# Mode rows loaded straight into TensorE's operand tiles, and two differences moved from VectorE to GpSimd

## The chip, the cores and the metric

The kernel runs on one core of a Trainium2 chip. The metric is the device time of one execution in microseconds. A core has TensorE (PE) for matmuls, VectorE (DVE), ScalarE (ACT) and GpSimd (POOL) for elementwise work, and SyncE (SP), which here only issues DMAs. Each engine works through its own instructions strictly in the order in which the program holds them.

## The reference

Four layers act on a sequence of 2048 steps and 512 channels: A, B, A, B, each on the layernorm of x and with a residual.

```
x = x + A(layernorm(x), k, v, shift_k, ssm_k, ssm_D)   # y = fftconv(kv, ssm_k) + kv*ssm_D;  q * y
x = x + B(layernorm(x), log_A_real, A_imag, C, log_dt, D_skip)
x = x + A(...)                                         # the same weights again
x = x + B(...)                                         # the same weights again
# inside B, for each of 512 channels and 128 modes:
P = exp((A * dt)[:, :, None] * arange(2048))           # A = -exp(log_A_real) + i*A_imag
K = 2 * einsum("dn,dnl->dl", C * dt, P).real           # the long kernel, then fftconv(u, K)
```

The kernel of B, K, is computed from modes: for each channel and mode there is a magnitude (the logarithm of |C|, and the decay per step) and a phase (the angle of C in turns, and the rotation per step).

## The kernel before, in words

The sequence is cut for an FFT of length 4096 that is done by matmuls with constant matrices (`w1`, `w2`, `mm`, `w4`). Work falls into three parts.

1. **The head**, written out directly. Four arrays `la`, `ai`, `cr`, `ci` (128 partitions x 512) hold the modes' parameters. From them the head makes four row arrays: decay `la`, rotation `ai`, phase `ph` and log magnitude `t2`. The helper `split(i, v, eng)` writes each of them as a high part (cast to fp32r on ScalarE) and a low part (the difference `v - high`, on the engine that is given) into a tile `hl`, and stores `hl` into the DRAM arrays `rows_d[0]` (phases) and `rows_d[1]` (magnitudes), in a layout in which PE can contract over parts and channels.
2. **The planned part**, called A below. Every instruction is recorded first and given an order by the class `Planner`, which plays the instructions through with a cost for each and takes at each step the one that can start first. Two generators are interleaved here. `stream()` makes K: 16 groups of modes (index `gi`), each in four taps `k`. `load_rows(gi)` fetches the rows of a group; `mags` multiplies them by tables and takes the exponential (tile `m`, PSUM tile `pm`); `angles` makes the phase in turns (PSUM tile `pa`), where DVE rounds it (`y`) and PE subtracts the rounded part; `waves` takes the sines (`tt`); `products` makes `xy` on GpSimd and `e2` on DVE; `contract` sums over modes (`pk`), scales (`ks`) and stores `kdram`. `diagonal()` does layer A: the products `prod` of k, v and the shift taps on GpSimd, summed on PE into `kv`, multiplied on DVE and stored to `kv_d`; the spectra (`kk`, `pf`, `zk`, `pu`, `pc`, stored in `spec`); row statistics of x (`xr`, `st`, `mv`, `nm`, `var`) and the convolution (`kab`, `vv`, `sw`, `pi`, `w`, `po`). `wk` is the pool of the stream's tiles.
3. **Three more layers**, after the plan's end at about 500 us: B, an A-type update without a new convolution (its result `ya_d` is read again), and B, in program order.

In `load_rows` two DMAs on SP's queue bring a group's phase rows and magnitude rows into a tile `raw` of type fp32; one copy on DVE makes `rw` of type fp32r from it, which PE reads as the stationary operand. `raw` and `rw` have two buffers each. Since `hl` was already of type fp32r when it was stored, the copy changes no bit that matters; it gives the tile the type that PE's operand needs. Group `gi + 1` is asked for when group `gi` starts.

The planner's `cost` knows a lock between DVE and GpSimd: for DVE it holds for an operation with two big operands in SBUF, and not for a copy. Its order is written out once, when the program is built; on the chip, nothing is reordered.

In the profile, L177 is the helper that records an instruction outside the plan, and L342 the line that writes out the planned ones; so the tiles' names tell the instructions apart, not the lines.

Of the kernel before, what the change touches and what calls it, by code (L numbers as in the profile page):

```python
# [9 lines left out]
F32 = mybir.dt.float32  # L10
F32R = mybir.dt.float32r
# [342 lines left out]
def kernel(ctx: ExitStack, tc: tile.TileContext, out, x_in, kv_in, ssmk_in, ssmd_in,  # L354
# [4 lines left out]
    V, S, G, T, Q = [planner.engine(e) for e in "VSGTD"]  # L359
    after = planner.after  # L360

    def sbuf(stack, name, side="left"):
        return stack.enter_context(tc.tile_pool(name=name, bufs=1, side=side, reuse_waits="tile"))
# [8 lines left out]
    rows_d = [dram.tile([NQ, 128, 4, 128], F32, name=f"rows_d{k}") for k in range(2)]  # L372
# [254 lines left out]
    def split(i, v, eng):  # L627
        k, r = divmod(i, 2)
        hl = nat.tile([128, 2, 4, 128], F32R, name="hl", tag="hl", bufs=4)
        S.copy(hl[:, 0], v)  # L630
        eng.tensor_sub(hl[:, 1], v, hl[:, 0])
        Q.dma_start(rows_d[k].rearrange("q (h r x) g n -> r (q h) x (g n)", h=2, r=2)[r]
                          .rearrange("a (c p) y -> a c (p y)", p=2),
                          hl.rearrange("p s g n -> p (s g n)").bitcast(F32))

    bits = lambda t_: t_.bitcast(I32)
    t0, t1, t2, t3, ph = [nat.tile([128, 4, 128], F32, name=n, tag=n) for n in ("t0", "t1", "t2", "t3", "ph")]
# [42 lines left out]
    V.tensor_mul(ph, ph, t0)  # L680
    V.scalar_tensor_tensor(ph, ph, -0.125, cr, op0=ALU.add, op1=ALU.mult)
    V.scalar_tensor_tensor(ph, ph, 0.25, ci, op0=ALU.add, op1=ALU.mult)
    split(1, ph, V)
    split(3, t2, V)
    S.activation(warm, t2[:, 0, 0:1], AF.Exp, scale=0.0)
    tabs = {}
    for key, w_, src in (("tg2", 32, tg2_in), ("tg1", 64, tg1_in), ("tt", 64, tt_in)):
# [15 lines left out]
    wk = sbuf(gctx, "wk")  # L703
# [10 lines left out]
    rows, ms, xys, pks, angs = {}, {}, {}, {}, {}  # L714
# [5 lines left out]
    def load_rows(gi):  # L720
        if gi in rows:
            return
        raw = wk.tile([128, 2, 128], F32, name="raw", tag="raw", bufs=2)
        q, g = divmod(gi, 4)
        for k in range(2):
            Q.dma_start(raw[:, k, :], rows_d[k][q, :, g, :])
        rows[gi] = wk.tile([128, 2, 128], F32R, name="rw", tag="rw", bufs=2)
        V.tensor_copy(rows[gi], raw)

    def mags(gi, s, col):  # L730
        pm = wide("pm")
# [79 lines left out]

    def taps():
        load_rows(0)
        load_rows(1)

        def exps(gi):
# [4 lines left out]
        for n in range(64 + LP + LC):  # L821
            gi, k = divmod(n, 4)
            if n < 64:
                if k == 0:
                    if gi > 0 and gi < 15:
                        load_rows(gi + 1)
                    if EORD == 1:
                        exps(gi)
                    elif EORD == 3 and gi % 2 == 0:
                        exps(gi)  # L830
                        exps(gi + 1)
                if n == XN:
                    root = normalizer(0, 16, lambda t: st0[:, t, :])
                    after(root, last_exp[0])
                    last_exp[0] = root
                    G.tensor_scalar(off, nm, -1.0, None, op0=ALU.mult)
                angles(gi, k)
                waves(gi, k)
            if 0 <= n - LP < 64:
                products(*divmod(n - LP, 4))  # L840
            m = n - LP - LC
            if 0 <= m < 64:
                contract(*divmod(m, 4))
                if m % 16 == 15:
                    todo.append(spectrum_quarter(1, m // 16, kdram, kp, zlast_k, 1))
            yield
# [381 lines left out]
```

## Time and profile before

| | |
|---|---|
| median of 3 runs | 748.78 us (744.72 to 751.23) |
| profiled execution: its own time | 749.08 us |
| profiled execution: span on the core | 747.2 us |
| mean granted TensorE clock | 0.877 |
| DVE instructions, POOL instructions | 918, 342 |
| head | about 0 to 34 us |
| planned part (A and the making of K) | to about 500 us |
| B, update, B | 500 to 747 us |

Rows of a timeline read: start in us, duration in us, engine, line, operation, output <- input, shape, count of merged instructions, and in brackets how long the engine sat idle before and what ended that. SPq is the queue of DMA issues on SP: its duration is the issue, together with what the queue waited for between merged issues.

### The profile page before, as it was taken

The numbers are of one execution on the slowest core, as the hardware profiler recorded it, in microseconds if no ns is written. First come the engines' busy times: TensorE is split into PE (matmuls) and PEld (weight loads), VectorE is DVE, ScalarE is ACT, GpSimd is POOL, SyncE is SP. The second block draws the span as 40 slices with busy tenths as digits, with TensorE's granted clock in tenths as the row PEclk, the third lists the DMA queues.
The fourth block names the chain that finished last, engine by engine and source line by source line (L and its number), as shares of the span: only waits on it lengthen the run. The fifth ranks groups of instructions, "written<-read, shape, count | busy, mean of one in ns | idle before, by whom it ended". The sixth has DMA issues, their size and how long they took to land. (4 is left out here: it accounts for less than half of the span.)

```text
span 747.2 us, 20838 instructions
## 1 busy us (share of the span) xinstructions
PE 553.5 (74%) x8568; PEld 307.6 (41%) x8568; DVE 508.5 (68%) x918; ACT 404.9 (54%) x768; POOL 350.1 (47%) x342
## 2 busy tenths in 40 slices
PE   1649688896798888798778789344798871589984
PEld 0114334333334434664354366122465530255662
DVE  6924965547653456578978659664588879978863
ACT  4118518655539878749445386237473326746341
POOL 3618866967756745432353053500554520254551
PEclk9988979998989659698897979876899995899998
DMA  9499858694465315565676745679686712068764
GB/s 245 121 228 236 260 153 237 182 245 125 130 197 181 132 50 150 180 210 163 199 191 232 226 124 182 171 253 277 200 283 228 253 66 104 2 212 261 250 207 93
DMA packets 74499, 138.97 MB, mean 186 GB/s; under 512 B 8092, under 2 KB 37156, under 8 KB 72356
## 3 DMA queue, kind: packets, MB, share of 16 engines
q1 hardware_dynamic: 73540, 135.21, 60.7%
q0 software_dynamic: 864, 2.43, 0.9%
q8 instruction: 68, 1.11, 0.6%
q14 instruction: 27, 0.22, 0.1%
HBM read 97.75 MB, written 39.85 MB: 184 GB/s over the span
## 5 line engine op out<-in xcount | busy, mean ns | idle before, releaser
L342 POOL TENSOR_TENSOR xy<-tt,m 128x512 f32<-128x512 f32 x128 | 148.5, 1185 | 143.9 <-ACT tt L342 64.0
L177 POOL TENSOR_TENSOR sw<-sw,kab 128x512 f32<-128x512 f32 x64 | 80.6, 1280 | 119.3 <-ACT sw L177 112.1
L342 PE MATMUL kv<-prod,minus 128*128 128x512 f32 x128 | 80.3, 720 | 9.3 <-DVE prod L342 7.1
L342 POOL TENSOR_TENSOR prod<-kvt 128x512 f32<-128x512 f32 x64 | 79.8, 1269 | 15.6 <-DMA kv_d<-prod 9.7
L342 ACT ACTIVATE m<-pm 128x1024 f32<-128x1024 f32 x48 | 46.9, 1026 | 57.8 <-PE pm L342 55.9
L342 PE MATMUL pf<-kk,w 64*128 64x512 f32 x128 | 45.0, 755 | 39.9 <-DMA kk<-ssmk_in 21.0
L342 ACT ACTIVATE ab<-pa 128x512 f32<-128x512 f32 x64 | 38.3, 599 | 61.0 <-PE pa L342 61.0
L342 DVE TENSOR_TENSOR e<-pa,m 128x512 f32<-128x512 f32 x64 | 43.6, 681 | 31.5 <-ACT pa L342 25.3
L177 DVE TENSOR_TENSOR vv<-pu,kab 128x512 f32<-128x512 f32 x64 | 40.9, 677 | 35.0 <-ACT sw L177 32.5
L177 ACT COPY ie<-pi 128x1024 f32<-128x1024 f32 x32 | 32.4, 1013 | 58.7 <-PE pi L177 58.7
L342 DVE TENSOR_SCALAR y<-pa 128x512 fp32r<-128x512 f32 x64 | 43.5, 682 | 30.0 <-PE pa L342 29.5
L177 PE MATMUL pf<-u,w 64*128 64x512 f32 (+1 forms) x136 | 40.1, 681 | 25.8 <-ACT u L177 15.8
L342 DVE STREAM_TRANSPOSE zk<-pf 128x512 f32<-128x512 f32 x64 | 41.4, 688 | 25.1 <-PE pf L342 25.1
L177 PE MATMUL pi<-vv,mm 64*64 64x128 f32 x1024 | 53.4, 276 | 1.1 <-DVE vv L177 1.1
L177 PE MATMUL pi<-sw,mm 64*64 64x128 f32 x1024 | 52.3, 270 | 1.7 <-issue 1.7
L342 PE MATMUL pa<-tt,rw 64*128 64x512 f32 x64 | 35.2, 554 | 23.1 <-DVE e L342 23.0
L342 PE MATMUL pa<-y,minus 128*128 128x512 f32 x64 | 41.9, 660 | 10.1 <-DVE y L342 10.1
L342 PE MATMUL pk<-xy,e 128*32 128x64 f32 x2048 | 47.3, 240 | 2.9 <-POOL xy L342 1.5
L177 ACT COPY sw<-pu 128x1024 f32<-128x1024 f32 x32 | 32.3, 1013 | 30.7 <-PE pu L177 30.7
L177 PE MATMUL pu<-zu,w 64*64 64x128 f32 x1024 | 37.2, 281 | 14.3 <-DVE zu L177 12.2
L342 PEld LDWEIGHTS pk<-xy,e 128*32 128x32 f32 x2048 | 36.0, 121 | 28.6 <-issue 19.8
L342 PE MATMUL pu<-zk,w 64*64 64x128 f32 x1024 | 40.0, 301 | 9.3 <-DVE zk L342 6.6
(134 smaller groups left out, 1181.1 us busy)
## 6 DMA issues: line engine op xcount, KB each, us to landing
kab<-spec SPq DMA_DIRECT2D x94, 512.0 KB, 4.6
spec<-pc SPq DMA_DIRECT2D x64, 256.0 KB, 4.3
kvt<-kv_in SPq DMA_DIRECT2D x32, 312.0 KB, 5.0
kk<-ssmk_in SPq DMA_DIRECT2D x32, 128.0 KB, 5.7
xr<-x_in SPq DMA_DIRECT2D x8, 512.0 KB, 6.6
kv_d<-prod SPq DMA_DIRECT2D x16, 256.0 KB, 3.9
kdram<-ks SPq DMA_DIRECT2D x64, 64.0 KB, 2.2
kk<-kdram SPq DMA_DIRECT2D x32, 128.0 KB, 2.8
```

The source lines that it names most:

```text
L177: op.ins = getattr(self.engines[key], name)(*a, **k).ins
L342: ins = getattr(self.engines[op.engine], name)(*a, **k).ins
```

## The change

The third argument of `split` is GpSimd instead of DVE for the rows `ph` and `t2`; the other two differences were on GpSimd already. `load_rows` lets its two DMAs write straight into `rw`, seen as fp32, and has neither `raw` nor the copy. `rw` has four buffers; `raw` and `rw` together had four.

```diff
-    split(1, ph, V)
-    split(3, t2, V)
+    split(1, ph, G)
+    split(3, t2, G)
...
     def load_rows(gi):
         if gi in rows:
             return
-        raw = wk.tile([128, 2, 128], F32, name="raw", tag="raw", bufs=2)
+        rows[gi] = wk.tile([128, 2, 128], F32R, name="rw", tag="rw", bufs=4)
         q, g = divmod(gi, 4)
         for k in range(2):
-            Q.dma_start(raw[:, k, :], rows_d[k][q, :, g, :])
-        rows[gi] = wk.tile([128, 2, 128], F32R, name="rw", tag="rw", bufs=2)
-        V.tensor_copy(rows[gi], raw)
+            Q.dma_start(rows[gi].bitcast(F32)[:, k, :], rows_d[k][q, :, g, :])
```

Because the planner plays the whole list again, the order of the planned part is a new one on every engine. In number, 16 copies and two differences leave DVE, two differences join GpSimd, and every other count stays.

On DVE, at the end of the head, stood the two differences (`hl_195` of the phases, `hl_199` of the magnitudes), then the transposes of layer A's first spectrum and the first copies:

```order
L177 SCALAR_TENSOR_TENSOR ph_148<-ph_148,ci_128 128x512
L177 TENSOR_TENSOR hl_195<-ph_148,hl_195 128x512
L177 TENSOR_TENSOR hl_199<-t2_146,hl_199 128x512
L342 STREAM_TRANSPOSE zk_229<-pf_232 128x512 x2
L342 STREAM_TRANSPOSE zk_229<-pf_238 128x512 x2
L342 SCALAR_TENSOR_TENSOR prod_234<-kv_236,kvt_233 128x512
L342 STREAM_TRANSPOSE zk_229<-pf_244 128x512 x2
L342 STREAM_TRANSPOSE zk_229<-pf_246 128x512 x2
L342 CAST rw_252<-raw_251 128x256
```

Now DVE goes from the phases to the transposes, and the two differences stand on GpSimd behind its earlier two, ahead of the first products:

```order
L177 TENSOR_TENSOR hl_165<-la_125,hl_165 128x512
L177 TENSOR_TENSOR hl_173<-ai_126,hl_173 128x512
L177 TENSOR_TENSOR hl_195<-ph_148,hl_195 128x512
L177 TENSOR_TENSOR hl_199<-t2_146,hl_199 128x512
L342 MEMSET tt0_223 128x8
L342 MEMSET tt0_223 128x16
L342 MEMSET tt1_224 128x8
L342 MEMSET tt1_224 128x16
L342 MEMSET tt2_225 128x8
L342 MEMSET tt2_225 128x16
L342 TENSOR_TENSOR kk_231<-kk_231,dr_230 1x32
L342 TENSOR_TENSOR prod_234<-kvt_233 128x512 x2
```

The first products on GpSimd (`prod`) thus stand behind all four differences, and DVE's transposes behind none.

On SP's queue the stores of `hl` are followed by loads for layer A and then by the first groups' rows. Before:

```order
L177 DMA rows_d1_103<-hl_199 8x16x1024
L342 DMA kk_245<-ssmk_in 64x1x512 x2
L342 DMA w2_108<-w2_in 128x512
L342 DMA kvt_247<-kv_in 64x1x1248 x2
L342 DMA kk_322<-ssmk_in 64x1x512 x2
L342 DMA xr_328<-x_in 64x1x2048
L342 DMA raw_251<-rows_d1_103 128x128
L342 DMA raw_253<-rows_d1_103 128x128
L342 DMA raw_251<-rows_d0_102 128x128
L342 DMA kv_d1_83<-prod_234 128x512
L342 DMA raw_253<-rows_d0_102 128x128
```

After the change the same loads stand there; the rows of a third group (`rw_301`) and the second half of `xr` have come ahead of the first groups' phase rows:

```order
L177 DMA rows_d1_103<-hl_199 8x16x1024
L342 DMA kk_245<-ssmk_in 64x1x512 x2
L342 DMA w2_108<-w2_in 128x512
L342 DMA kvt_247<-kv_in 64x1x1248 x2
L342 DMA xr_325<-x_in 64x1x2048
L342 DMA kk_319<-ssmk_in 64x1x512 x2
L342 DMA rw_251<-rows_d1_103 128x128
L342 DMA rw_252<-rows_d1_103 128x128
L342 DMA rw_301<-rows_d1_103 128x128
L342 DMA dr_318<-ssmd_in 1x128
L342 DMA xr_325<-x_in 64x1x2048
L342 DMA rw_251<-rows_d0_102 128x128
```

Further on, on DVE, two small operations on the row statistics, `nm` and `var` (128x16, from SBUF to SBUF), had a copy of rows behind them:

```order
L342 TENSOR_TENSOR e2_374<-pa_364,m2_353 128x512
L342 TENSOR_SCALAR nm_115<-mv_111 128x16
L342 TENSOR_SCALAR var_113<-mv_111 128x16
L342 TENSOR_SCALAR y_387<-pa_386 128x512
L342 TENSOR_TENSOR e2_390<-pa_370,m2_353 128x512
L342 TENSOR_SCALAR y_392<-pa_391 128x512
L342 CAST rw_406<-raw_405 128x256
```

They are still there, with a product `e2` between them, and the copy is gone:

```order
L342 TENSOR_SCALAR nm_115<-mv_111 128x16
L342 TENSOR_TENSOR e2_370<-pa_360,m2_349 128x512
L342 TENSOR_SCALAR var_113<-mv_111 128x16
L342 TENSOR_SCALAR y_383<-pa_382 128x512
L342 TENSOR_TENSOR e2_386<-pa_366,m2_349 128x512
```

## The prediction

> **What bounds the kernel now.** I read the profile page first (shares), then the planned part in stretches of 25 us, then the timelines of DVE, GpSimd, SP and PE where the edited instructions stand, and the groups of instructions by form for their prices.
>
> ```profile
> PE 553.5 (74%) x8568; PEld 307.6 (41%) x8568; DVE 508.5 (68%) x918; ACT 404.9 (54%) x768; POOL 350.1 (47%) x342
> 75.00:100.00 25.00, 14.87 (x207) 7.32 (x202) 22.48 (x26) 10.48 (x27) 17.91 (x18) 0.86 0.72 212
> 150.00:175.00 25.00, 24.70 (x254) 10.48 (x252) 12.96 (x21) 15.71 (x27) 18.58 (x20) 1.00 0.88 231
> ```
>
> No engine is full over the span. The second and third rows are two stretches of the same stage (busy us of PE, its loads, DVE, ACT, POOL; then the clock and the DMA share). In the good one PE is busy 24.7 of 25 us; in the bad one 14.9, and there DVE alone is nearly full, with 26 instructions. A bad stretch of this kind is a stall on DVE, so the question is what DVE does in it. The last instruction's chain is no help here: it can be followed back to 448 us only. But the three layers behind the planned part start from its last result, so what this part gains the end gains.
>
> The first place is the end of the head.
>
> ```profile
> 22.19 10.35 DVE L177 TENSOR_TENSOR hl<-ph,hl 128x512 fp32r<-128x512 f32 x1 [0.69 <-ACT hl L177]
> 32.46 0.73 DVE L177 TENSOR_TENSOR hl<-t,hl 128x512 fp32r<-128x512 f32 x1
> 10.39 1.25 POOL L177 TENSOR_TENSOR hl<-la,hl 128x512 fp32r<-128x512 f32 x1
> 21.97 2.48 POOL L342 TENSOR_TENSOR prod<-kvt 128x512 f32<-128x512 f32 x2
> 24.63 7.36 POOL L342 TENSOR_TENSOR prod<-kvt 128x512 f32<-128x512 f32 x6
> 53.52 8.71 POOL L342 TENSOR_TENSOR prod<-kvt 128x512 f32<-128x512 f32 x7 [9.71 <-DMA kv_d<-prod]
> 19.92 13.93 SPq L177 DMA_DIRECT2D rows_d<-hl  x3
> 33.94 4.37 SPq L342 DMA_DIRECT2D kk<-ssmk_in  x2
> 43.51 2.23 SPq L342 DMA_DIRECT2D raw<-rows_d  x3
> 53.85 1.94 ACT L342 ACTIVATE m<-pm 128x1024 f32<-128x1024 f32 x2 [31.17 <-PE pm L342]
> ```
>
> The phase difference takes 10.35 us, its twin 0.73. It lasts as long as GpSimd's run of products from 21.97 us, and ends when the run does. SP's queue stands behind it: the last stores of `hl` leave at 33 us, the loads behind them follow, the rows are asked for from 43.5 us, and ACT, idle for 31 us, gets its first exponential at 53.85. GpSimd too waits 9.7 us for a store that stands in the same queue.
>
> The second place is the copy that makes `rw`.
>
> ```profile
> L342 DVE CAST rw<-raw 128x256 fp32r<-128x256 f32 x16 | 29.7, 1854 | 5.2 <-DMA raw<-rows_d 5.2
> 85.36 9.56 DVE L342 CAST rw<-raw 128x256 fp32r<-128x256 f32 x1
> 85.13 2.48 POOL L342 TENSOR_TENSOR prod<-kvt 128x512 f32<-128x512 f32 x2
> 87.58 4.55 POOL L342 TENSOR_TENSOR xy<-tt,m 128x512 f32<-128x512 f32 x4
> 92.30 2.47 POOL L342 TENSOR_TENSOR prod<-kvt 128x512 f32<-128x512 f32 x2
> 95.67 0.76 PE L342 MATMUL pa<-tt,rw 64*128 64x512 f32 x1 [7.55 <-DVE e L342]
> 100.73 1.18 POOL L342 TENSOR_TENSOR xy<-tt,m 128x512 f32<-128x512 f32 x1 [5.70 <-PE pk L342]
> 174.37 7.02 DVE L342 CAST rw<-raw 128x256 fp32r<-128x256 f32 x1
> 182.77 1.98 PE L342 MATMUL pu<-zk,w 64*64 64x128 f32 x32 [6.10 <-DVE zk L342]
> 190.14 2.35 POOL L342 TENSOR_TENSOR xy<-tt,m 128x512 f32<-128x512 f32 x2 [8.89 <-PE pk L342]
> 198.25 6.70 DVE L342 CAST rw<-raw 128x256 fp32r<-128x256 f32 x1
> 205.70 2.02 PE L342 MATMUL kv<-prod,minus 128*128 128x512 f32 x2 [4.94 <-DVE prod L342]
> 208.79 0.24 POOL L342 TENSOR_TENSOR kk<-kk,dr 1x32 f32<-1x32 f32 x1 [3.74 <-DMA kk<-ssmk_in]
> ```
>
> Sixteen copies take 29.7 us, but three of them hold 23.3 (9.56 + 7.02 + 6.70). Each again lasts through a run of GpSimd without a gap. Behind it PE runs dry and waits for DVE, and when DVE is free GpSimd waits for PE or a load: the time is lost to all three.
>
> **The change, part by part, against the profiled execution's 749.08 us** (span 747.2 and 1.9 around it; the median shown is 0.3 below).
>
> *Start.* On GpSimd the two differences cost 1.25 us each by the row of its own difference. The last ends near 22.2 + 2 x 1.25 = 24.7 us, where DVE's ended at 33.2: the stores leave 8.5 us earlier, and the loads, the rows and the first exponential behind them. What is late next is GpSimd's first product, 3.1 us (24.7 + 0.4 of small work against 21.97); its cover is the 9.71 us in which GpSimd waits later. Without that cover the gain is 5.4. Above, it could be 12.3:
>
> ```profile
> SPq L342 <- PE pf L342: 21.8, 15, 3.8
> ```
>
> The longest of SP's waits for a forward matmul, 3.8 us, lies in the pair of loads at 33.94 us, whose matmuls DVE's stall kept back. I take 8.5, as the queue's order up to the rows is nearly the same.
>
> *The three stalls.* Without the copy DVE goes on to the next `e`, `zk` or `prod`. PE idled 7.55 + 6.10 + 4.94 = 18.6 us behind them, GpSimd 5.70 + 8.89 + 3.74 = 18.3. Not all of it goes, because PE waits for DVE there in any case.
>
> ```profile
> PE pa L342 <- DVE e L342: 23.0, 16, 7.5
> SPq L342 <- DVE rw L342: 24.0, 9, 9.0
> ```
>
> By the first row (us in total, times, longest) such a wait is 23.0/16 = 1.4 us, so 18.6 - 3 x 1.4 = 14.3; I take 14, with 0 below (if GpSimd's queue bounds the stretch) and 18.6 above. The second row is SP's queue held by the copies; now a load into `rw` waits for PE's last use four groups back, which is further away than the two of before, so I add no wait.
>
> *The other thirteen copies* are 29.7 - 23.3 = 6.4 us of DVE, whose cover is its own idle time (12 of 25 us in the good stretch). I take 0, between 0 and 6.4. DVE's 5.2 us of waiting for rows becomes PE's at the same moment, behind the same DMAs: 0. The 32 DMAs stay as they are.
>
> *Where a stall can go next.* `nm` and `var`, too, are DVE operations from SBUF to SBUF, in the same stretch.
>
> ```profile
> 120.55 2.31 POOL L342 TENSOR_TENSOR xy<-tt,m 128x512 f32<-128x512 f32 x2 [4.68 <-ACT tt L342]
> 121.90 0.99 DVE L342 TENSOR_SCALAR nm<-mv 128x16 f32<-128x16 f32 x1
> 122.81 0.16 DVE L342 TENSOR_SCALAR var<-mv 128x16 f32<-128x16 f32 x1
> 126.66 1.03 DVE L342 CAST rw<-raw 128x256 fp32r<-128x256 f32 x1
> ```
>
> Before, `nm` came in a short run and lost 0.8 us. Of the eight copies up to 205 us three met a long run, of 7.8 us in the mean: 3/8 x 7.8 = 2.9. I charge 3, between -0.8 (a gap) and 19.1 (both meet the longest).
>
> The Trainium skill, in "SBUF — State Buffer", section "Who interferes with whom", says that whichever of the two engines holds the shared port keeps it for one whole instruction. By that rule a wait would end with one GpSimd operation, about 1.2 us; the row of 9.56 us outlasts eight big ones, so the trace does not agree. By the rule the charge for `nm` would be near 0 and the sum 3 us better.
>
> *Sum:* 8.5 + 14 + 0 - 3 = 19.5 us; 749.1 - 19.5 = **729.6 us**.
>
> **The rivals.** *A, only the start is gained.* GpSimd used the stalls to run ahead, and is busy 17.9 and 18.6 of 25 us in the rows above; if its queue is the real bound, the stalls come back as its own waits. Against it: it then idles 18.3 us. 749.1 - 8.5 = 740.6.
>
> *B, the clock comes on top.* Behind each stall PE's clock is low.
>
> ```profile
> 95.00:100.00 5.00, 3.30 (x27) 1.34 (x30) 4.11 (x7) 0.00 (x0) 0.03 (x1) 0.50 0.28 87
> 100.00:105.00 5.00, 4.80 (x58) 2.39 (x51) 2.86 (x8) 1.93 (x4) 4.27 (x5) 0.67 0.58 146
> 180.00:185.00 5.00, 2.23 (x33) 1.89 (x33) 3.79 (x5) 0.19 (x1) 1.25 (x2) 0.68 0.30 106
> 185.00:190.00 5.00, 5.00 (x41) 1.97 (x41) 1.86 (x3) 2.36 (x7) 0.00 (x0) 0.63 0.89 258
> 205.00:210.00 5.00, 4.30 (x7) 1.79 (x7) 3.07 (x5) 1.75 (x5) 1.26 (x3) 0.57 0.59 170
> 210.00:215.00 5.00, 4.13 (x72) 1.97 (x70) 1.38 (x2) 2.42 (x4) 3.97 (x5) 0.74 0.84 246
> ```
>
> PE's busy time times what the clock lacks is 3.2 + 2.6 + 2.9 = 8.7 us. With no stall taken off for waits that stay: 749.1 - 8.5 - 18.6 - 8.7 = 713.3. Against it: PE's clock also falls where DVE does not stall.
>
> *C, the stall moves on: slower.* Besides `nm` and `var` the normalizer has five more small SBUF operations on DVE, behind its root. If k of the seven meet long runs, 7.8 us each come back; with 22.5 gained, the kernel is slower from k = 3, and at k = 4 it is 749.1 - 22.5 + 31.2 = 757.8. Against it: the five stand together, so that one wait serves them all, and GpSimd is filled with gaps by then.
>
> *D, the new order eats the gain.* The planner's order is new on all engines, and PE's idle time differs by stretch from 0.3 to 10.1 us in the two rows above. Over 18 stretches, 1.1 us more in each is the whole 19.5: about 749, nothing that can be measured. Against it: the rows of the head and of the first groups are nearly in the old order.
>
> **How the numbers follow.** My forecast has 0.60, A 0.15, B 0.10, C 0.07, D 0.08. The time is the first's, 729.6, its own range 720 to 740. B's end (713) and D's (749) bound the whole: 712 to 750 leaves out C, and the edges of B and D. A measurement of this kernel can tell about 1% from no change, so "faster" is below 741.6 and "slower" above 756.6. The forecast gives 0.58 to faster and 0.02 to same; A, whose 740.6 lies near the edge, 0.08 and 0.07; B 0.10 to faster; D 0.01, 0.06 and 0.01; C 0.07 to slower. Faster 0.77, same 0.15, slower 0.08.
>
> **What would show it.** In the changed profile: no `rw<-raw` group; two differences of about 1.25 us on POOL that end near 24.7 us; SP's stores of `hl` done by 26 us; ACT's first exponential near 45 us instead of 53.85; between 75 and 225 us no stretch in which DVE is full and PE below 16 of 25 us; and the load of x behind the plan near 483 us; before it is this piece of the chain that ended last (start, duration):
>
> ```profile
> 502.30 6.42 DMA x<-x_d
> ```
>
> I am wrong in the stalls if such a stretch appears with `nm`, `var` or another small DVE operation of several us in it; wrong in the start if the first exponential stays behind 50 us; wrong in the carrying over if both are as said and the plan still ends near 500 us.

## The result and the profile after

The changed kernel takes 714.44 us (median of 4 runs, 713.95 to 715.50) where the kernel before takes 749.76 (4 runs, 744.72 to 751.23): the ratio is 0.9542, interval 0.9495 to 0.9590. The gain is 35.3 us, against 19.5 forecast. The profiled execution has a span of 712.1 us, and the mean granted clock rises from 0.877 to 0.898. Ratios and their intervals, here and below, are worked out from the fast runs alone, so they can differ a little from the quotient of the medians.

The first page line (busy time, share, instructions), and the two stretches of 25 us that were shown of before, with one more (busy us of PE, its loads, DVE, ACT, POOL; the clock; the DMA share; GB/s):

```profile
PE 542.0 (76%) x8568; PEld 299.9 (42%) x8568; DVE 470.6 (66%) x900; ACT 405.4 (57%) x768; POOL 351.1 (49%) x344
```

```profile
75.00:100.00 25.00, 22.33 (x213) 8.94 (x214) 16.58 (x31) 12.64 (x22) 22.20 (x22) 1.00 0.95 292
150.00:175.00 25.00, 24.33 (x361) 12.57 (x362) 15.80 (x26) 20.01 (x51) 22.71 (x22) 1.00 0.65 202
200.00:225.00 25.00, 19.92 (x355) 11.71 (x347) 10.41 (x16) 22.54 (x51) 20.13 (x21) 0.74 0.52 170
```

The stretch from 75 us, in which DVE was full and PE busy for 14.87 us at a clock of 0.86, now has PE at 22.33 at full clock and DVE at 16.58. DVE lost 38 us of "busy" time over the span, of which the removed instructions would have needed about 6 (16 copies of 0.28 us where nothing held them, two differences of 0.73 at most): the rest was waiting that the profile counts as busy.

The instructions of the prediction's steps, from the timelines of POOL, SP's queue, ACT and DVE of the changed kernel (start, duration):

```profile
22.42 1.26 POOL L177 TENSOR_TENSOR hl<-ph,hl 128x512 fp32r<-128x512 f32 x1 [2.48 <-ACT hl L177]
23.65 1.26 POOL L177 TENSOR_TENSOR hl<-t,hl 128x512 fp32r<-128x512 f32 x1
...
20.28 5.22 SPq L177 DMA_DIRECT2D rows_d<-hl  x3
...
43.96 1.03 ACT L342 ACTIVATE m<-pm 128x1024 f32<-128x1024 f32 x1 [21.10 <-PE pm L342]
...
102.50 0.17 DVE L342 TENSOR_SCALAR nm<-mv 128x16 f32<-128x16 f32 x1
104.72 0.99 DVE L342 TENSOR_SCALAR var<-mv 128x16 f32<-128x16 f32 x1
```

The differences take 1.26 us each and end at 24.9; the stores of `hl` are issued by 25.5; the first exponential comes at 43.96 instead of 53.85; `nm` and `var` lose 0.8 us together. In the chain that ended last the load of x behind the plan stands 34.8 us earlier than the 502.30 of before, so the whole gain lies ahead of it:

```profile
467.53 6.41 DMA x<-x_d
```

### The profile page after: what moved, and what is told of

The parts are those of the page before. It is cut to its first block, busy times and chain, and to the rows that moved or that the text cites. A ratio compares the mean times of both kernels' runs of the same rounds, so it can differ in the third digit from the quotient of the medians.

```text
span 712.1 us, 20816 instructions
## 1 busy us (share of the span) xinstructions
PE 542.0 (76%) x8568; PEld 299.9 (42%) x8568; DVE 470.6 (66%) x900; ACT 405.4 (57%) x768; POOL 351.1 (49%) x344
## 4 chain that ended last, share of the span: by engine, by line
PE 34%; DVE 24%; ACT 15%; issue 7%; DMA 5%; POOL 2%; SPq 0%; DVEq 0%; ACTq 0%; POOLq 0%
PE pf L342 4%; PE kv L342 4%; PE pi L342 4%; PE pa L342 4%; PE pu L342 3%; PE pi L177 3%; ACT tt L342 3%; DMA kab<-spec 3%; PE pf L177 3%; PE pk L342 2%; DVE w L177 2%; ACT m L342 2%; DVE zu L177 2%; PE pu L177 2%; DVE vv L177 2%
## 5 line engine op out<-in xcount | busy, mean ns | idle before, releaser
L342 PE MATMUL kv<-prod,minus 128*128 128x512 f32 x128 | 75.4, 680 | 2.9 <-DMA kvt<-kv_in 1.9
L342 DVE STREAM_TRANSPOSE zk<-pf 128x512 f32<-128x512 f32 x64 | 41.6, 691 | 27.5 <-PE pf L342 27.4
L342 PE MATMUL pk<-xy,e 128*32 128x64 f32 x2048 | 45.2, 231 | 5.4 <-POOL xy L342 1.9
L342 PEld LDWEIGHTS pk<-xy,e 128*32 128x32 f32 x2048 | 34.0, 115 | 30.2 <-issue 20.7
L177 DVE STREAM_TRANSPOSE zu<-pf 128x512 f32<-128x512 f32 x64 | 41.5, 688 | 4.9 <-PE pf L177 4.7
L342 PE MATMUL pa<-y,minus 128*128 128x512 f32 x64 | 37.2, 584 | 9.0 <-DVE y L342 8.9
```

The costliest lines, as they stand in the source:

```text
L177: op.ins = getattr(self.engines[key], name)(*a, **k).ins
L342: ins = getattr(self.engines[op.engine], name)(*a, **k).ins
```

## The experiments

Because the planner plays its list again after every edit, an edit also brings a new order. In the kernels called "old order" below, the planner sees what it saw in the kernel before, and the edit is made when the instruction is written out; DVE, PE, ACT, POOL and SP then hold their rows in the order of before, with only the named rows taken out or put in. Times are medians of 4 runs unless another count is given; the kernel before took 746.5 to 747.6 beside them.

**1. The start alone.** Both differences on GpSimd, copies as before, old order.

```diff
-    split(1, ph, V)
-    split(3, t2, V)
+    split(1, ph, G)
+    split(3, t2, G)
```

> The two differences on GpSimd, the copies kept, and the order of the planned part held as before (same rows on every engine but the two). Theory P (a DVE operation that needs the port shared with GpSimd waits through GpSimd's run, and the gain is these waits): the 10.35 us wait of the phase difference goes, the first exponential starts about 10 us earlier as in the changed kernel (43.96 us), the three long copies stay: 735 to 741 us. Theory O (the new order of the plan brings most of the gain): 745 us or more. My own term for the start was 8.5 us, which gives 741.

738.36 us, ratio 0.9844 (0.9775 to 0.9914): 9 us (by the interval, 6 to 17). Timeline of ACT and of DVE in this kernel:

```profile
45.33 1.94 ACT L342 ACTIVATE m<-pm 128x1024 f32<-128x1024 f32 x2 [22.46 <-PE pm L342]
...
76.44 9.55 DVE L342 CAST rw<-raw 128x256 fp32r<-128x256 f32 x1
166.91 7.21 DVE L342 CAST rw<-raw 128x256 fp32r<-128x256 f32 x1
189.90 6.72 DVE L342 CAST rw<-raw 128x256 fp32r<-128x256 f32 x1
```

The first exponential is 8.5 us earlier, and the three stalls come back at the same places and with the same length. They belong to those places, not to chance.

**2. The copies alone.** Rows loaded straight into `rw`, the planner still counting sixteen copies, none written out; differences on DVE, old order.

```diff
-        raw = wk.tile([128, 2, 128], F32, name="raw", tag="raw", bufs=2)
+        rows[gi] = wk.tile([128, 2, 128], F32R, name="rw", tag="rw", bufs=4)
+        raw = Stand(rows[gi].bitcast(F32)[:, :, :], f"raw{gi}", 2)   # counted, no memory
...
-        V.tensor_copy(rows[gi], raw)
+        V.tensor_copy(rows[gi], raw).left_out = True
```

> The rows are loaded straight into rw (four buffers), the differences stay on DVE, and the order is held as before: the planner still counts the 16 copies, and only writes none of them out. Theory P: the 10.35 us difference at the start stays, the three long waits of 23.3 us go with the copies: 722 to 730 us, a gain near 25 rather than the 14 of my sum. Theory O: 745 us or more. Theory W (it is the step between DMA and matmul that counts, not the port): as P.

716.99 us, ratio 0.9575 (0.9495 to 0.9656): 30 us, twice what the forecast gave to the stalls and 5 us more than I expected here. The differences still wait on DVE, only otherwise divided; DVE's and POOL's timelines:

```profile
24.10 2.81 DVE L193 TENSOR_TENSOR hl<-ph,hl 128x512 fp32r<-128x512 f32 x1 [0.68 <-ACT hl L193]
26.83 8.06 DVE L193 TENSOR_TENSOR hl<-t,hl 128x512 fp32r<-128x512 f32 x1
...
26.33 0.69 POOL L361 TENSOR_TENSOR kk<-kk,dr 1x32 f32<-1x32 f32 x1
26.98 7.36 POOL L361 TENSOR_TENSOR prod<-kvt 128x512 f32<-128x512 f32 x6
```

**3. The same sixteen copies, in a form that does not wait.** Everything as before, but the copy is a multiplication by one that also writes out its sum.

```diff
-        V.tensor_copy(rows[gi], raw)
+        acc = wk.tile([128, 1], F32, name="acc", tag="acc", bufs=2)
+        V.tensor_scalar(rows[gi], raw, 1.0, 0.0, op0=ALU.mult, op1=ALU.add, accum_out=acc)
```

> The copy stays on DVE at its old place, but as a multiply by 1 that also writes its sum out, a form which I take to need no second port; order and differences as before. Theory P: each copy takes about 0.4 us and none over 1 us, and the time is that of the run without copies to within 4 us: 722 to 732 us. Theory W: the copy still stands between load and matmul and on DVE, so 745 to 750 us. If this form needs the port too, there are again copies of several us and the time stays near 749.

722.82 us, ratio 0.9658 (0.9591 to 0.9725). The group of DVE, and four of the five instances that follow the place of the first long stall:

```profile
L342 DVE TENSOR_SCALAR_CACHE_REDUCE rw<-raw 128x256 fp32r<-128x256 f32 x16 | 6.5, 409 | 5.2 <-DMA raw<-rows_d 5.2
...
116.10 0.41 DVE L342 TENSOR_SCALAR_CACHE_REDUCE rw<-raw 128x256 fp32r<-128x256 f32 x1
...
163.84 0.41 DVE L342 TENSOR_SCALAR_CACHE_REDUCE rw<-raw 128x256 fp32r<-128x256 f32 x1
179.14 0.41 DVE L342 TENSOR_SCALAR_CACHE_REDUCE rw<-raw 128x256 fp32r<-128x256 f32 x1
209.65 0.41 DVE L342 TENSOR_SCALAR_CACHE_REDUCE rw<-raw 128x256 fp32r<-128x256 f32 x1
```

All sixteen last 0.41 us, and 24.5 us are gained with the copies still between the load and the matmul. So it is the copies' waiting that costs most, not that there is a copy; whether the step itself costs some of the 6 us to experiment 2, whose interval touches this one's, was not settled. The Trainium skill, in "SBUF — State Buffer", section "Who interferes with whom", says that copies and casts can take the read and write port that DVE shares with GpSimd, and the form that writes out its accumulator cannot; these rows agree.

The same rows give the price of a stall. The kernel before has these five copies at 85.36, 126.66, 174.37, 198.25 and, from its timeline of DVE,

```profile
236.73 0.32 DVE L342 CAST rw<-raw 128x256 fp32r<-128x256 f32 x1
```

and this kernel has the first of them at 85.77. Before lags by -0.4, 10.6, 10.5, 19.1 and 27.1 us: the stall of 9.56 us cost 11.0, that of 7.02 cost 8.6 and that of 6.70 cost 8.0.

What this lag of 27.5 us consists of can be read between the first and the last of these copies (columns as above), first before, then here:

```profile
85.36:236.73 151.37, 122.48 (x1310) 56.38 (x1312) 89.80 (x118) 83.83 (x171) 105.37 (x101) 0.90 0.65 185
126.66:174.37 47.71, 44.18 (x498) 20.06 (x494) 24.25 (x39) 29.49 (x62) 39.46 (x40) 0.96 0.78 207
...
85.77:209.65 123.88, 113.77 (x1309) 52.69 (x1312) 67.86 (x122) 84.00 (x171) 105.19 (x101) 0.97 0.78 226
116.10:163.84 47.74, 44.20 (x498) 20.07 (x495) 23.66 (x41) 29.56 (x62) 39.36 (x40) 0.96 0.79 215
```

The second row of each kernel is the part in which no copy waits long: there the two take the same time. Over the whole, PE idles 28.9 us before (151.37 - 122.48) and 10.1 here, which is 18.8 us of the lag. The other 8.7 are busy time of PE (122.48 against 113.77) for the same matmuls at a lower clock: busy time times clock is about 110 us in both.

**4. Both, in the old order.** Edits 1 and 2 together.

> Both parts of the change in the old order: no copies, four buffers, the differences on GpSimd. Theory P: the gains of the two single parts add up and the order is worth little: 710 to 718 us beside 714.4 of the changed kernel. Theory O: 730 us or more, and the difference to 714.4 is what the new order brings.

708.99 us, ratio 0.9463 (0.9402 to 0.9524): 38 us, about the sum of 9 and 30, and 1 us below the range that I expected. Its median is 5 us below that of the changed kernel; with the second kernel of experiment 5, which has the same time, it is the fastest here that does the whole computation.

**5. Three of the copies put back, and the other thirteen.** On top of 4; the copies go into a tile that nobody reads, so they can cost DVE's time only.

```diff
+        op = V.tensor_copy(rows[gi], raw)
+        if gi in (3, 6, 7):        # the other kernel: not in (3, 6, 7)
+            op.instead = (junk, rows[gi].bitcast(F32))
+        else:
+            op.left_out = True
```

> Both parts in the old order (709.0 us), and put back on DVE only the three copies that waited long (groups 3, 6 and 7), writing into a tile that nobody reads: no result waits for them. Theory P with its price (a stalled DVE delays everything behind it by the stall's full length and a little more for the clock): the three last about 9.5, 7 and 6.7 us again and cost 25 to 28 us: 733 to 738 us. My sum's price (what PE idled behind them less its usual waits, 14 us): 723. Theory W (the step between load and matmul): 709 to 712.

> As the run with three copies put back, but the other thirteen: none of them met a long run of GpSimd. Theory P: none lasts over 1.5 us, and they cost what the run without copies was better than the run with copies that need no port, at most 6 us: 709 to 715 us. If one of them now falls on a long run, it shows as a copy of several us and costs its length.

With the three: 734.24 us, ratio 0.9856 (0.9782 to 0.9930), 25 us more than without. With the thirteen: 708.43 us, ratio 0.9486 (0.9411 to 0.9561), nothing. DVE's timeline of the kernel with three:

```profile
72.73 9.56 DVE L363 CAST junk<-rw 128x256 f16<-128x256 f32 x1
162.72 7.23 DVE L363 CAST junk<-rw 128x256 f16<-128x256 f32 x1
187.27 6.71 DVE L363 CAST junk<-rw 128x256 f16<-128x256 f32 x1
```

Three instructions, each of which takes 0.3 us where nothing holds it, are worth 25 us.

**6. The new order again.** The changed kernel itself, beside the two of 5.

> The changed kernel itself, beside the others on one chip, for what the new order is worth. Theory P: 712 to 716 us; the old order with both parts (709.0) is better by 3 to 7 us, and would lie between 706 and 711 here. If the order is worth nothing, 709.

715.54 us, ratio 0.9613 (0.9531 to 0.9695). The new order is about 6 us slower than the old one, both times that the two were compared (714.44 against 708.99, and 715.54 against the 708.43 of the kernel with thirteen copies); the intervals still touch.

**7. Why do three copies wait through a run, and thirteen not?** A small kernel that computes nothing of the reference: one DVE operation becomes ready amid a run of GpSimd's.

> Not the reference's work: forty-eight short sections that measure the port, output zero. In each GpSimd makes a run of seven products (128x512, about 8.5 us), or the same run with one small add behind a semaphore already met in its middle, or 28 small products (128x128), or seven memsets; one DVE operation becomes ready 1 to 2 us into the run: a copy from SBUF to SBUF, an add of two SBUF tiles, a multiply that writes its sum out, or a product of a PSUM and an SBUF tile (128x256). Theory P: copy and add last 6 to 8 us in the long run (to its end, not to the end of one product), the multiply with its sum and the product from PSUM 0.3 to 0.5 us. If the port goes over at every product's end, copy and add last 1.5 us at most. With the small add in the run they end there, at about 2 to 4 us, if a semaphore wait is what lets DVE in. Beside memsets I expect the add to be free and the copy not.

Amid seven products of 128x512 the copy and the sum of two SBUF tiles lasted 0.29 to 1.55 us, to the end of one product, not of the run, also where a small addition on all partitions stood in it: my expectation was wrong. The multiplication that writes out its sum, and the product with an operand in PSUM, waited in no case (0.42 to 0.43 us). Beside memsets the sum did not wait and the copy did (2.0 to 2.9 us, until the last of the seven). Amid 28 products of 128x128 the copy took 0.39 to 0.44 us, but the sum lasted 8.1 to 8.6 us all three times. It was let in at the 20th or 22nd product, which took 0.74 us where the others take 0.45, about 3 us ahead of the run's end (DVE, then POOL):

```profile
89.19 8.17 DVE L77 TENSOR_TENSOR y<-z,x 128x256 fp32r<-128x256 f32 x1 [1.25 <-ACT z L55]
...
96.94 0.74 POOL L69 TENSOR_TENSOR run<-a,b 128x128 f32<-128x128 f32 x1
97.64 3.33 POOL L69 TENSOR_TENSOR run<-a,b 128x128 f32<-128x128 f32 x8
```

**8. Is it the form of GpSimd's operations?** The same with products in the forms of `prod` and `xy`, and a mixture that has two additions in the form of `kk` between them.

> A small kernel that does not do the reference's work (its output is zero): 48 sections, in each of which one DVE operation becomes ready while GpSimd works through eight products of 512 elements without a gap (about 10 us). GpSimd's products have four forms: plain (two whole rows), those of `prod` (an operand repeated over the row), those of `xy` (pieces of 32 elements), and a mixture in the order that stands behind the longest stall (two `prod`, four `xy`, two `prod`). DVE's operation is a copy of 128x256 or a difference of 128x512, either waiting for ACT or standing directly behind a DVE operation that waited; each at three offsets. What is open is why the copies in the kernel wait through a whole run (9.56 us), while the copies of the first small kernel waited for one product (0.55 to 1.42 us). Theory F, GpSimd's form of access decides: plain sections 0.3 to 1.6 us again, `prod`, `xy` or mixture sections 4 to 10 us. Theory B, it matters that the copy stands behind another operation of DVE and waits for nothing itself: only the sections of that kind last 4 to 10 us, in every form. Theory M, the moment decides: long and short waits in all forms, differing by offset. Where all 48 stay below 1.8 us, none of these is it, and the question stays open.

In 47 of 48 sections the DVE operation lasted at most 1.66 us, in every form and also directly behind another DVE operation: theories F and B fall. The 48th started while such a small addition ran, and lasted to the run's end (DVE, then POOL):

```profile
498.44 7.92 DVE L89 TENSOR_TENSOR w<-a,xz 128x512 fp32r<-128x512 f32 x1
...
498.34 0.24 POOL L83 TENSOR_TENSOR run<-kvt 1x32 f32<-1x32 f32 x1
```

In the other eleven sections with such additions DVE was ready ahead of the first of them. This suggests a `kk` ahead of DVE's operation, in the same run of GpSimd, as the cause. In the kernel before, all four long waits had one (POOL's timeline; the 10.35 us began at 22.19, the three copies at 85.36, 174.37 and 198.25):

```profile
21.76 0.24 POOL L342 TENSOR_TENSOR kk<-kk,dr 1x32 f32<-1x32 f32 x1
...
84.92 0.24 POOL L342 TENSOR_TENSOR kk<-kk,dr 1x32 f32<-1x32 f32 x1
...
174.03 0.24 POOL L342 TENSOR_TENSOR kk<-kk,dr 1x32 f32<-1x32 f32 x1
...
194.93 0.24 POOL L342 TENSOR_TENSOR kk<-kk,dr 1x32 f32<-1x32 f32 x1
```

The copies and `nm` that met a run without one ahead of them (seven in that trace) waited 0.83 us at most; the second difference, whose run had one, began when that run was at its end. `kk` adds one row of 32 numbers on a single partition.

**9. One small operation ahead of eight products, in several forms.**

```diff
+    G.tensor_add(dst[0:1, 1:33], a[0:1, 0:32], b[0:1, 0:32])              # first: 1x32
+    G.tensor_add(dst[:, 1:33], a[:, 0:32], b[:, 0:32])                    # first128: 128x32
+    G.tensor_scalar(dst[0:1, 1:33], a[0:1, 0:32], 2.0, None, op0=ALU.mult) # scalar: 1x32
```

> A small kernel that does not do the reference's work (its output is zero): 40 sections, in each of which GpSimd works through eight plain products of 128x512 without a gap (about 10 us) and one DVE operation (a copy of 128x256 or a difference of 128x512, behind another DVE operation) becomes ready at one of four moments. The sections differ in one small operation: none; an addition of 1x32 (the form of GpSimd's `kk`) ahead of the products; the same on 128 partitions; a multiplication by a number, 1x32, ahead of them; the addition of 1x32 behind the fourth product. Theory K, suggested by the kernel's traces, in which every copy that waited long met a run that had such a `kk` in it and every copy that waited for one operation met a run without: behind the small addition the port stays with GpSimd until its run ends, so the sections with it ahead show waits of 3 to 9 us and those without 0.3 to 1.7; with it behind the fourth product only the latest of the four moments waits long. The sections on 128 partitions and with one operand tell whether the single partition or the second operand matters. Rival T, only the moment matters (the DVE operation must start within about 0.1 us of a short operation's start): all sections below 1.8 us except by chance.

DVE's copies at the earliest moment, in the sections without the small operation, with 1x32, with 128x32, and with the one-operand 1x32, in this order:

```profile
9.07 1.30 DVE L82 CAST w<-x 128x256 fp32r<-128x256 f32 x1
...
30.14 8.76 DVE L82 CAST w<-x 128x256 fp32r<-128x256 f32 x1
...
51.51 0.28 DVE L82 CAST w<-x 128x256 fp32r<-128x256 f32 x1
...
73.03 8.83 DVE L82 CAST w<-x 128x256 fp32r<-128x256 f32 x1
```

So it is throughout: the 16 sections with an operation on a single partition ahead lasted 5.73 to 9.23 us, to the run's end, with one operand as with two; the 8 on 128 partitions and the 8 with none 0.28 to 1.64. In the 8 with the addition behind the fourth product, DVE was ready ahead of it each time, and none waited long (0.38 to 1.65). Theory K holds but for the sections with the addition behind the fourth product, which could not test it; and what matters is the single partition, not the second operand. Numbers of partitions between 1 and 128 were not tried.

**10. Does it hold in the kernel? Without the additions.** The kernel with three copies of 5, and no `kk` additions.

```diff
-            G.tensor_add(kv[0:1, 0], kv[0:1, 0], d)
+            G.tensor_add(kv[0:1, 0], kv[0:1, 0], d).left_out = True
```

> The kernel of e6_three_copies (order of before, rows loaded directly, both differences on GpSimd, the copies of groups 3, 6 and 7 put back into a tile that nobody reads) without the 32 small additions `kk` on GpSimd: the carry of the state is not added, and so this part of the computation is left out. DVE, PE and ACT keep their order but for one pair of transposes in the head, and three stores of `hl` stand a few loads later in SP's queue, which may cost the start 1 to 4 us. Theory K (a small addition lets GpSimd's run keep the port to its end): the three copies take 0.3 to 1.6 us each instead of 9.56, 7.23 and 6.71, and the time falls from 734 to 705 to 716. Rival T (the additions have nothing to do with it): at least two of the three still take 4 to 10 us, and the time stays at 726 to 738.

708.56 us, ratio 0.9502 (0.9440 to 0.9564), as without the three copies. They are still there (group of DVE):

```profile
L363 DVE CAST junk<-rw 128x256 f16<-128x256 f32 x3 | 2.5, 849 | 0.0
```

**11. Nothing of the change, and `kk` on all partitions.** The kernel before, old order, five rounds. (The rows of the two spectra share one tile here, so that some additions take the other spectrum's row; their number, shape and place are as described.)

```diff
+    drs = cpool.tile([128, 128], F32, name="drs")      # zero, but for row 0
+    nc.gpsimd.memset(drs, 0.0)
...
-            G.tensor_add(kv[0:1, 0], kv[0:1, 0], d)
+            G.tensor_add(kv[0:1, 0], kv[0:1, 0], d).instead = (kv[:, 0], kv[:, 0], da)
```

> The kernel before with nothing of the change in it: DVE makes the 16 copies and both differences. Only the small additions `kk` on GpSimd run over all 128 partitions instead of one (the other 127 rows of their second operand are zero, so the sum is the same); the order is that of before on every engine, with one memset more ahead. Theory K (an operation of GpSimd on a single partition leaves the port with GpSimd until its run ends, and this is what made the copies and the difference wait): the differences in the head take 0.5 to 1.7 us each instead of 10.35, the sixteen copies 0.3 to 1.7 us each, 8 to 14 us in total instead of 29.7; the start gains 6 to 9 us and the stalls about 25, so the time is 708 to 722, as fast as the changed kernel or nearly so. Rival (the single partition does not matter in the kernel, and leaving the additions out helped only by breaking up the runs): copies of 4 to 10 us stay, the time is 735 to 755.

712.68 us (6 runs), ratio 0.9563 (0.9508 to 0.9618): as much as the whole change gains, with all copies and both differences on DVE. Groups of DVE and of POOL, and DVE's timeline at the end of the head:

```profile
L344 DVE CAST rw<-raw 128x256 fp32r<-128x256 f32 x16 | 9.6, 600 | 3.0 <-DMA raw<-rows_d 3.0
L344 POOL TENSOR_TENSOR kk<-kk,drs 128x32 f32<-128x32 f32 x32 | 8.3, 266 | 34.4 <-DMA kk<-kdram 29.4 <-DMA kk<-ssmk_in 2.8 <-PE pa L344 2.2
...
23.09 1.59 DVE L177 TENSOR_TENSOR hl<-ph,hl 128x512 fp32r<-128x512 f32 x1 [0.69 <-ACT hl L177]
24.61 1.75 DVE L177 TENSOR_TENSOR hl<-t,hl 128x512 fp32r<-128x512 f32 x1
```

Sixteen copies take 9.6 us instead of 29.7, the first difference 1.59 instead of 10.35, and the 32 additions cost what they cost before (8.3 us; 8.1 on one partition).

## Why the prediction was right and wrong

- **The time.** 714.4 us lies outside the 720 to 740 that the forecast gave as its own range. The whole range, 712 to 750, holds it only because it reaches down to rival B.
- **The start: right in size.** 8.5 us forecast, 9 measured by experiment 1 (6 to 17 by its interval), and every sign of it came: 1.26 us for each difference, the stores by 25.5, the first exponential at 45.33 alone and 43.96 in the changed kernel.
- **The three stalls: right place, half the size.** This is the step that failed: "Not all of it goes, because PE waits for DVE there in any case", which made 14 us of 18.6, with nothing added for the clock. Experiment 5 measured 25 us for the three alone, experiment 2 measured 30 for all copies. By the traces of experiment 3 a stall cost more than its own length: 27.5 us of lag (11.0 + 8.6 + 8.0) for 23.3 us of stalls. PE's idle time fell by 18.8, the whole 18.6 and not 14, and 8.7 more came from the same matmuls at a higher clock. So 18.6 was no bound. (The 1.4 us taken for a usual wait, moreover, is a mean that has the stall's own 7.5 in it.)
- **Rival B was the right account of the stalls.** Its two terms, 18.6 of idle time and 8.7 for the clock, came out as 18.8 and 8.7, though it was given one chance in ten. That its total of 713.3 lies so near 714.4 is in part luck: it has no term for the new order, which took back about 6 us. The clock was not tried by itself; that it accounts for the 8.7 rests on the two traces of experiment 3.
- **The other thirteen copies: right.** Nothing forecast, nothing measured (experiment 5).
- **`nm` and `var`: too dear.** 3 us charged on top of the 0.8 that `nm` lost before; after the change `var` loses the same 0.8, so the charge should have been 0. It took 3 in 8 as the chance that a long run is met. Length alone does not decide: with a `kk` ahead in the run the waits were long, and neither `nm` before nor `var` after had one. For such runs the rule that the prediction had set aside, in the Trainium skill's "SBUF — State Buffer", section "Who interferes with whom", that the port is held for one whole instruction, was the better guide: without a single-partition operation ahead, the waits amid big products were at most one operation long. For the runs with one, it does not hold; 9.56 us is what the trace showed.
- **Rival D, in small.** The new order takes back about 6 us (experiment 6), about 0.3 in each of 18 stretches where D put 1.1. Which wait makes it was not followed.
- **Rivals A and C fall.** GpSimd's queue did not hand the stalls back, and no stall went to the normalizer's small operations.
- **The sum by the measured terms:** 9 for the start, 25 to 30 for the copies, about 6 back for the order: 28 to 33 of the 35 us. When the change was measured again in experiment 6 it gained 32 (747.59 to 715.54), so the rest is within what the runs scatter. The prediction had seen the pattern (long waits through runs without a gap) and taken it for how the port works everywhere. The cause stood in the same timeline, 0.4 us ahead of the two longest waits, in a row of 0.24 us.

What stays open: why a single-partition operation has this effect, and on how many partitions it ends; why some of the long waits ended at another such operation (the difference of 2.81 us in experiment 2 ended at the `kk` at 26.33; of the four long waits before, three ended at a `kk` that was the last row of its run) and passed others on the way; and the waits of 8.1 to 8.6 us amid 28 products of 128x128 in experiment 7, which had no single-partition operation ahead. There must be another way into a long wait than a `kk`.

## What to carry to other kernels

When a cheap DVE operation lasts many times its own length, list GpSimd's instructions around several such cases, long and short, and ask what stands in the one kind of run and not in the other; here it was a row of 0.24 us on one partition, and running it on all partitions (experiment 11) was worth as much as the whole change, while data loaded in its final type, a form that writes out its accumulator and a move to GpSimd are ways around it. Price a stall in the engine that feeds PE at PE's whole idle time behind it and its slower clock (here 18.8 + 8.7 us, more than the stalls' own 23.3), not at the idle time less what is usual. Where a planner sets the order, test an edit with the order held still.

## What the runs showed of the hardware that was not expected

- Behind an operation of GpSimd on one partition, a DVE copy or difference waited until GpSimd's run of products ended: 16 sections of 16 lasted 5.73 to 9.23 us, against at most 1.64 in 16 of 16 with the operation on 128 partitions or none. The operation itself costs nearly the same in both forms (0.26 and 0.27 us each in the kernels of before and of experiment 11).
- A copy of 128x256 on DVE took 0.28 us free, 0.41 in the form that writes out its sum, and up to 9.56 held.
- The sum of two SBUF tiles did not wait beside GpSimd's memsets (0.42 to 0.43 us), while a copy waited until the last memset of the run (2.0 to 2.9 us).
- A sum of two SBUF tiles waited 8 us through some 20 products of 128x128 without a single-partition operation ahead, and was let in about 3 us before their run ended; a copy in the same place took 0.39 to 0.44 us.
